# The first weight load of a decode block: 32 rows by four instead of sixteen by eight

## The chip, the core and the metric

The kernel runs on one core of a Trainium2 chip. Five engines work on their own instruction streams: TensorE (PE; its weight loads are shown apart as PEld), VectorE (DVE), ScalarE (ACT), GpSimd (POOL) and SyncE (SP), which here issues nearly all transfers. Sixteen DMA engines move data between the device memory and the core's on-chip memory of 128 partitions; one transfer is shared out over them in packets. The metric is the device time of one execution in microseconds (us), as the median of several runs.

## What is computed

One decode step for eight sequences: normalisation of x, attention over the last 2,048 positions of a cache (32 query heads, 8 key/value heads of 128), and a gated feed-forward block whose output gates the attention's.

```python
x  = A_x                                   # 8 x 1 x 512, bf16
xn = layernorm(x)
W  = min(4096, max(256, Sk // 4))          # Sk = 8192: W = 2048
q  = xn @ wq                               # wq: 512 x 4096, 32 heads of 128
k, v = the last W rows of the caches       # caches: 8 x 8 x 8192 x 128
p  = softmax(q k^T / sqrt(128))
s  = (p v) @ wo                            # wo: 4096 x 512
h  = sigmoid(xn @ w_gate) * (xn @ w_up)    # 512 x 1792 each
g  = silu(h @ w_down)                      # 1792 x 512
out = x + s * g
```

## The kernel before

All loads but that of x go through one helper (lines 112 to 115) and so through SP's queue, in program order; x comes in three pieces on ScalarE's queue (line 125). SP waits only where a load reuses a buffer. K tiles, the weights of the feed-forward block and wo share a ring of three buffers, V tiles a ring of four; `issue_loads` (line 216) issues the next load of a list ordered by when its tile is due, as soon as the buffer before it has been released.

The order on SP's queue is: wq (two loads, lines 131 and 132), K 0 and K 1 at once, K 2 when the q projection has released wq's buffer, then the other K loads (eight of 4 MB in all), the V loads (sixteen of 2 MB), gate and up weights, the down weight, and wo in six pieces that get smaller.

wq is 512 x 4096 in bf16: 8 KB a row. Its first 128 rows are contraction tile 0 and come in the first load, one row to a partition. The other 384 rows come in the second load, three adjacent rows to a partition. Which row stands on which partition is free, as long as normed x is brought into the same order. Line 131 cuts the first 128 rows into 8 by 16 and swaps them, so that partition 8e+i takes row 16i+e. The transfer's source then has 16 outer rows, 8 KB apart, by 8 inner rows, 128 KB apart, of 8 KB each; the destination is 128 partitions.

Normed x (8 x 512, `xn_bf`) is built on VectorE and ScalarE from line 244 on, after x has landed. Lines 265 to 269 copy its first 128 columns into `xn0_bf` in the order of the partitions; for the other contraction tiles a strided view is enough. Four PE transposes (line 272) put the columns on partitions, line 297 copies them into `xnT_sb`, and `q_projection` (line 412) multiplies: two groups of 16 matmuls (line 421), contraction tile 0 first. So the first four matmuls need the first load alone, the fifth needs the second load.

From there `q_out` brings q into the block form `qz_sb` (ScalarE and VectorE, lines 435 to 452). A loop over steps (line 685) then runs, each with its own lag: VectorE's 32x32 transposes of K tiles in place (line 480, 64 of them), the score matmuls (line 495), maxima, exponentials on ScalarE, the turning and spreading of the probabilities, and the products with V (line 625). Near the end come the feed-forward block (lines 370 and 396) and the output projection with wo (line 739), which consumes wo's pieces as they land, then two VectorE instructions and the store.

The K loads have a source of 32 outer rows by 4 (lines 144 to 149: sequence and head by a quarter of the rows), the V loads too (lines 160 to 165: 32 groups of rows by 4 heads). The second wq load, gate, up, down and wo have 128 outer rows, one to a partition.

Of the kernel before, what the change touches and what calls it, by code (L numbers as in the profile page):

```python
# [10 lines left out]
def kernel(  # L11
# [14 lines left out]
    P = 128  # L26
# [85 lines left out]
    def load(dst, src, q=None):  # L112
        if q is None:
            q = nc.sync
        q.dma_start(out=dst, in_=src)  # L115

    def k_tile(shape, name):
        return kring.tile(shape, bf16, name=name, tag="kring", align_bytes=ALIGN)
# [5 lines left out]
    for c0, c1 in ((0, 2), (2, 3), (3, 4)):  # L124
        nc.scalar.dma_start(
            out=x_bf[:, P * c0 : P * c1],
            in_=A_x.flatten_outer_dims()[:, P * c0 : P * c1],
        )

    wq_sb = k_tile([P, KT, Hq * Dh], "wq_sb")  # L130
    load(wq_sb[:, 0], A_wq[:P].rearrange("(i e) n -> e i n", e=16))
    load(
        wq_sb[:, 1:].rearrange("p kt n -> p (kt n)"),
        A_wq[P:].rearrange("(p kt) n -> p (kt n)", kt=KT - 1),
# [81 lines left out]
    def issue_loads():  # L216
# [36 lines left out]
        out=rstd[:], in_=mv[:, 1:2], func=AF.Sqrt, bias=eps_t[:], scale=1.0  # L253
    )
    nc.vector.reciprocal(out=rstd[:], in_=rstd[:])
    xn_bf = ppool.tile([B, D], bf16, name="xn_bf", tag="pp")
    nc.vector.tensor_scalar(
        out=xn_bf[:],
# [5 lines left out]
    )  # L264
    xn0_bf = work.tile([B, P], bf16, name="xn0_bf")
    nc.vector.tensor_copy(  # L266
        out=xn0_bf[:].rearrange("b (e i) -> b e i", e=16),
        in_=xn_bf[:, :P].rearrange("b (i e) -> b e i", e=16),
    )
    xnT_ps = psum_a.tile([P, KT, B], bf16, name="xnT_ps", tag="acc_ps")  # L270
    for kt in range(KT):
        nc.tensor.transpose(  # L272
            out=xnT_ps[:, kt, :],
            in_=xn0_bf[:] if kt == 0 else xn_bf[:B, P + kt - 1 :: KT - 1],
# [3 lines left out]
    for kt in range(KT):  # L278
        nc.tensor.transpose(
            out=xnU_ps[:, kt, :], in_=xn_bf[:B, kt::KT], identity=ident[:B, :B]  # L280
        )
    x2_ps = psum1.tile([NCOL * 32, DC], f32, name="x2_ps", tag="misc")
    for c in range(NCOL):
# [21 lines left out]
        out=HR[:],  # L305
        in_=ident[:].rearrange("m (h q r) -> m h r q", q=NQ, r=rep),
# [6 lines left out]
        out=Qm[:],  # L313
        in_=ident[:].rearrange("m (h q r) -> m q h r", q=NQ, r=rep),
# [6 lines left out]
        out=Hm[:],  # L321
        in_=ident[:].rearrange("p (a gl) -> p gl a", gl=GL),
# [6 lines left out]
    for j in range(GL):  # L329
        for gg in range(NG):  # L330
            g = NG * gg + j // 2
            nc.gpsimd.tensor_copy(
                out=spread[:, gg, j % 2, :, j], in_=ident[:, 32 * g : 32 * g + PP]
# [5 lines left out]
        out=rows_of[:],  # L339
        in_=ident[:].rearrange("p (a m) -> p m a", m=w),  # L340
# [5 lines left out]
        out=Sel[:], in_=rows_of[:].rearrange("p (g c r) -> p c g r", g=GL, c=NCH)  # L346
# [5 lines left out]
    for gg in range(NG):  # L352
        rows = slice(32 * gg, 32 * (gg + 1))
        cols = slice(NE * GL * rep * gg, NE * GL * rep * (gg + 1))
        for e in range(NE):
            nc.gpsimd.tensor_copy(
                out=pick[rows, e, cols].rearrange("p (h d) -> p h d", d=NE)[:, :, e],
                in_=ident[rows, 32 * gg : 32 * gg + GL * rep],
# [326 lines left out]
    for t in range(PV_LAG + NSLOT):  # L685
# [18 lines left out]
        if u >= NJ and u % NJ == 0:  # L704
            i = u // NJ - 1
# [47 lines left out]
    for c in range(NCOL):  # L753
        queues[c].dma_start(
            out=out.flatten_outer_dims()[:, DC * c : DC * (c + 1)],
            in_=y_bf[32 * c : 32 * c + B, :],
# [31 lines left out]
```

## Time and profile before

| | |
|---|---|
| time, median of 3 runs (us) | 199.28 (199.24, 199.28, 204.17) |
| the profiled execution (us) | 199.27 |
| its span, first to last instruction (us) | 197.5 |
| mean TensorE clock granted | 0.912 |
| PE busy | 102.0 us, 52% of the span |
| VectorE busy | 105.7 us, 53% |
| ScalarE busy | 30.9 us, 16% |
| GpSimd busy | 4.7 us, 2% |
| read from device memory | 81.01 MB, 410 GB/s over the span |
| first wq load (1 MB), issue to landing | 7.0 us |
| second wq load (3 MB), issue to landing | 13.5 us |
| K loads (4 MB each), median | 20.1 us |

How to read the profile: times in it are from the span's start. The page cuts the span into 40 slices and gives for each the busy tenths of every engine, the granted TensorE clock, the DMA engines' busy share and what they moved. The chain follows the work that ended last back to the start. The view of windows gives, for stretches of one's own choice, each engine's busy time with the number of its instructions, then the granted clock, the DMA share and GB/s; packets are counted where they start, so short windows can show shares over 1. The list of queues gives packets, MB and the time of the packets as a share of 16 engines. The time from issue to landing of a load contains its wait behind the loads ahead of it in the queue.

### The profile page before, as it was taken

Reading aid. Unit: us, or ns where it says so; the run is one execution under the profiler, and the core shown is the slowest. Engines: PE = TensorE matmul, PEld = TensorE weight load, DVE = VectorE, ACT = ScalarE, POOL = GpSimd, SP = SyncE. Lnnn points to the kernel's source line nnn. Section 1 sums busy time; section 2 is a strip of 40 time slices with the busy share of each in tenths; the row PEclk is TensorE's granted clock in tenths of the full one; section 3 lists DMA queues with packets and bytes.
Section 4 is the critical chain, followed back from the end, with each engine's and each line's share of the span. In section 5 each row is a group of like instructions: output and inputs, shape, how many; then the busy total and the mean of one; then the engine's idle time right before and its main releaser. Section 6 shows DMA issues by size and latency. Waiting matters only on the chain.

```text
span 197.5 us, 1899 instructions
## 1 busy us (share of the span) xinstructions
PE 102.0 (52%) x754; PEld 36.0 (18%) x754; DVE 105.7 (53%) x150; ACT 30.9 (16%) x70; POOL 4.7 (2%) x26
## 2 busy tenths in 40 slices
PE   0026003333333327423495989848634894596653
PEld 0012001110101112100021222322211231233551
DVE  0244199998999999799969924423100010040401
ACT  2004132000000073200011034421111114002000
POOL 8000000000000000000000000000000000000000
PEclk9999999999999999955579799999999798569999
DMA  5999999999999999899999999999999999999991
GB/s 142 365 450 425 425 425 425 425 428 418 433 504 431 431 425 425 378 445 448 425 428 425 425 425 428 446 435 425 435 425 425 428 427 433 444 421 422 433 396 36
DMA packets 5128, 81.14 MB, mean 411 GB/s; under 512 B 616, under 2 KB 768, under 8 KB 1152
## 3 DMA queue, kind: packets, MB, share of 16 engines
q1 hardware_dynamic: 5056, 81.01, 96.8%
q8 instruction: 6, 0.10, 0.2%
q10 hardware_dynamic: 64, 0.01, 0.0%
q14 instruction: 2, 0.02, 0.0%
HBM read 81.01 MB, written 0.01 MB: 410 GB/s over the span
## 4 chain that ended last, share of the span: by engine, by line
DMA 63%; DVE 23%; PE 10%; SPq 1%; issue 1%; ACT 1%; DVEq 0%
DMA k_sb<-in_A_k_cache_dram 25%; DVE k_sb L480 18%; DMA wgu_sb<-in_B_w_up_dram 13%; DMA wo_sb<-in_A_wo_dram 12%; DMA v_sb<-in_A_v_cache_dram 7%; DMA wq_sb<-in_A_wq_dram 7%; PE acc_ps L625 3%; DVE pt_bf L543 2%; PE pT_ps L556 2%; PE o_ps L651 2%; PE q_ps L421 2%; PE s_ps L495 1%; DVE mx L509 1%; SPq L115 1%; DVE o_sb L660 0%
## 5 line engine op out<-in xcount | busy, mean ns | idle before, releaser
L480 DVE STREAM_TRANSPOSE k_sb<-k_sb 128x1024 f32<-128x1024 f32 x64 | 73.7, 1209 | 6.4 <-DMA k_sb<-in_A_k_cache_dram 6.3
L495 PE MATMUL s_ps<-k_sb,qz_sb 128*32 128x512 bf16 x256 | 30.1, 570 | 53.7 <-DVE k_sb L480 47.9
L625 PE MATMUL acc_ps<-v_sb,pT_sb 128*64 128x512 bf16 x256 | 37.3, 421 | 10.9 <-DMA v_sb<-in_A_v_cache_dram 10.7
L660 DVE TENSOR_TENSOR o_sb<-o_ps,rden 16x512 bf16<-16x512 f32 (+2 forms) x6 | 3.0, 504 | 47.4 <-PE o_ps L651 47.4
L495 PEld LDWEIGHTS <-qz_sb 128*32 128x32 bf16 x256 | 8.6, 116 | 78.3 <-issue 55.2
L639 ACT COPY acc_sb<-acc_ps 128x512 f32<-128x512 f32 x16 | 9.4, 585 | 82.5 <-PE acc_ps L625 82.5
L625 PEld LDWEIGHTS <-pT_sb 128*64 128x64 bf16 x256 | 12.7, 116 | 30.9 <-DMA v_sb<-in_A_v_cache_dram 15.4
L651 PE MATMUL o_ps<-acc_sb,Sel 128*16 128x512 f32 (+2 forms) x48 | 16.5, 494 | 3.4 <-ACT acc_sb L639 3.4
L577 DVE TENSOR_SCALAR pT_sb<-pc_bf,Hm 128x1024 bf16<-128x1024 bf16 x16 | 6.6, 477 | 5.3 <-PE acc_ps L625 5.3
L523 ACT ACT_TABLE_LOAD x1 | 1.3, 1283 | 39.8 <-DVE nm L517 39.8
L651 PEld LDWEIGHTS o_ps<-acc_sb,Sel 128*16 128x16 f32 x48 | 4.7, 105 | 14.4 <-issue 8.1
L509 DVE TENSOR_REDUCE mx<-s_ps 128x1 f32<-128x512 f32 x8 | 5.3, 662 | 3.2 <-PE s_ps L495 3.2
L556 PE MATMUL pT_ps<-pt_bf,spread 128*128 128x512 bf16 x16 | 6.0, 500 | 1.2 <-DVE pt_bf L543 0.7
L739 PE MATMUL a_ps<-wo_sb,o_sb 128*32 128x256 bf16 x64 | 4.5, 273 | 3.6 <-DMA wo_sb<-in_A_wo_dram 3.4
L452 ACT COPY qz_sb<-qT_sb 32x32 bf16<-32x32 bf16 x20 | 4.8, 242 | 8.1 <-DVE qT_sb L440 7.9
L370 PE MATMUL d_ps<-wgu_sb,xnU_sb 128*32 128x448 bf16 x32 | 3.4, 573 | 4.9 <-DMA wgu_sb<-in_B_w_up_dram 2.6
L272 PE MATMUL xnT_ps<-ident,xn_bf 8*128 8x8 bf16 x4 | 0.3, 167 | 10.9 <-DVE xn_bf L266 10.9
L523 ACT ACTIVATE p_bf<-s_ps,nm 128x512 bf16<-128x512 f32 x8 | 5.4, 685 | 0.0
L421 PE MATMUL q_ps<-wq_sb,xnT_sb 128*32 128x512 bf16 x32 | 3.8, 626 | 2.9 <-DMA wq_sb<-in_A_wq_dram 2.9
L564 ACT CAST pc_bf<-pT_ps 128x512 bf16<-128x512 f32 x8 | 4.5, 586 | 5.0 <-DVE pt_bf L543 2.8
L543 DVE STREAM_TRANSPOSE pt_bf<-p_bf 128x512 bf16<-128x512 bf16 x8 | 4.9, 666 | 0.0
L244 DVE CAST x_f<-x_bf 8x512 f32<-8x512 bf16 x1 | 0.4, 415 | 8.1 <-DMA x_bf<-in_A_x_dram 8.1
(64 smaller groups left out, 40.3 us busy)
## 6 DMA issues: line engine op xcount, KB each, us to landing
k_sb<-in_A_k_cache_dram SPq DMA_DIRECT2D x8, 4096.0 KB, 20.1
v_sb<-in_A_v_cache_dram SPq DMA_DIRECT2D x16, 2048.0 KB, 16.1
wq_sb<-in_A_wq_dram SPq DMA_DIRECT2D x1, 3072.0 KB, 13.5
wgu_sb<-in_B_w_gate_dram SPq DMA_DIRECT2D x1, 1792.0 KB
wgu_sb<-in_B_w_up_dram SPq DMA_DIRECT2D x1, 1792.0 KB, 24.7
wd_sb<-in_B_w_down_dram SPq DMA_DIRECT2D x1, 1792.0 KB
wo_sb<-in_A_wo_dram SPq DMA_DIRECT2D x1, 1536.0 KB
wo_sb<-in_A_wo_dram SPq DMA_DIRECT2D x1, 1152.0 KB, 33.4
```

Of the source, the lines that this page charges most:

```text
L421: nc.tensor.matmul(q_ps[gg][32 * gl : 32 * (gl + 1), :], lhsT=xnT_sb[:, kt, :], rhs=wq_sb[:, kt, h0 : h0 + HW], start=(kt == 0), stop=(kt ...
L452: nc.scalar.copy(out=out, in_=in_)
L480: nc.vector.transpose(out=kw, in_=kw)
L495: nc.tensor.matmul(s_tiles[i][32 * g : 32 * (g + 1), :], lhsT=qz_sb[:, hb, h, 2 * a + e, :], rhs=kT[:, :, a, h, :, e], start=(n == 0), sto ...
L509: nc.vector.reduce_max(out=mx_of[hb][:, kq : kq + 1], in_=s_tiles[i][:], axis=AX.X)
L523: nc.scalar.activation(out=p_bf[:, :, kq], in_=s_tiles.pop(NK * hb + kq)[:].rearrange("p (o c j) -> p c j o", o=2, j=NC), func=AF.Exp, bia ...
L543: nc.vector.transpose(out=pt[:, w * n : w * (n + 1)], in_=p_bf[:, w * n : w * (n + 1)])
L556: nc.tensor.matmul(pT_ps[:], lhsT=spread[:, gg, y].rearrange("p k g -> p (k g)"), rhs=pt[:, c, y, :], start=(y == 0), stop=(y == 1), skip_ ...
L577: nc.vector.tensor_scalar(out=pT_of[hb, gg][:, :, gl, :], in0=pc, scalar1=Hm[:, gl : gl + 1], scalar2=None, op0=ALU.mult,)
L625: nc.tensor.matmul(acc_tiles[i][w * c : w * (c + 1), :], lhsT=pT[:, GL * rep * ch : GL * rep * ch + w], rhs=v_tiles[i][:, ch : ch + NCH, : ...
L639: nc.scalar.copy(out=acc_sbs[i // NSUM][:, i % NSUM], in_=acc_tiles.pop(i)[:])
L651: nc.tensor.matmul(o_ps[rows, :n, :], lhsT=Sel[:, c].rearrange("p g r -> p (g r)"), rhs=acc_sb[:, :, Dh * c : Dh * (c + 1)], start=(c == 0 ...
```

## The change

Two numbers go from 16 to 32. The first wq load cuts its 128 rows into 4 by 32 before it swaps them: partition 4o+i takes row 32i+o, and the source has 32 outer rows, 8 KB apart, by 4 inner rows, 256 KB apart. `xn0_bf` is written in the same order. The bytes, the size of a row, the number of instructions and the order of all work stay as they are; each engine's instructions stand in the same order in both programs.

```diff
     wq_sb = k_tile([P, KT, Hq * Dh], "wq_sb")
-    load(wq_sb[:, 0], A_wq[:P].rearrange("(i e) n -> e i n", e=16))
+    load(wq_sb[:, 0], A_wq[:P].rearrange("(i e) n -> e i n", e=32))
     load(
         wq_sb[:, 1:].rearrange("p kt n -> p (kt n)"),
...
     xn0_bf = work.tile([B, P], bf16, name="xn0_bf")
     nc.vector.tensor_copy(
-        out=xn0_bf[:].rearrange("b (e i) -> b e i", e=16),
-        in_=xn_bf[:, :P].rearrange("b (i e) -> b e i", e=16),
+        out=xn0_bf[:].rearrange("b (e i) -> b e i", e=32),
+        in_=xn_bf[:, :P].rearrange("b (i e) -> b e i", e=32),
     )
```

## The prediction

> **What bounds the kernel now.** I read the page's slices first, then its chain and its list of transfers.
>
> ```profile
> DMA  5999999999999999899999999999999999999991
> GB/s 142 365 450 425 425 425 425 425 428 418 433 504 431 431 425 425 378 445 448 425 428 425 425 425 428 446 435 425 435 425 425 428 427 433 444 421 422 433 396 36
> ...
> q1 hardware_dynamic: 5056, 81.01, 96.8%
> ...
> DMA 63%; DVE 23%; PE 10%; SPq 1%; issue 1%; ACT 1%; DVEq 0%
> ...
> wq_sb<-in_A_wq_dram SPq DMA_DIRECT2D x1, 3072.0 KB, 13.5
> ...
> wq_sb<-in_A_wq_dram SPq DMA_DIRECT2D x1, 1024.0 KB, 7.0
> ```
>
> The 16 DMA engines are full from the first slices to the last but one, on one queue. PE and VectorE stand at 52 and 53% of the span. So the end is set by bytes over rate, and a hole at the start of the stream moves everything after it. The only slices well under 425 GB/s while the queue has work are the first two: there lies the load that the change touches, 1 MB that lands 7.0 us after its issue.
>
> Then the stages, cut where that load's packets go round (one round is one packet on each of 16 engines). The last two columns are the DMA share and GB/s.
>
> ```profile
> 2.38:2.74 0.36, 0.00 (x0) 0.00 (x0) 0.00 (x0) 0.36 (x1) 0.30 (x2) 1.00 1.19 364
> 2.74:3.19 0.45, 0.00 (x0) 0.00 (x0) 0.00 (x0) 0.45 (x1) 0.45 (x4) 1.00 0.96 328
> 3.19:3.67 0.48, 0.00 (x0) 0.00 (x0) 0.00 (x0) 0.15 (x1) 0.48 (x5) 1.00 1.05 274
> 3.67:4.27 0.60, 0.00 (x0) 0.00 (x0) 0.00 (x0) 0.00 (x0) 0.54 (x4) 1.00 1.06 221
> 4.27:4.90 0.63, 0.00 (x0) 0.00 (x0) 0.00 (x0) 0.00 (x0) 0.59 (x5) 1.00 0.94 208
> 4.90:5.46 0.56, 0.00 (x0) 0.00 (x0) 0.00 (x0) 0.00 (x0) 0.53 (x4) 1.00 1.19 278
> 5.46:6.04 0.58, 0.00 (x0) 0.00 (x0) 0.00 (x0) 0.00 (x0) 0.00 (x0) 1.00 0.94 198
> 6.04:6.55 0.51, 0.00 (x0) 0.00 (x0) 0.00 (x0) 0.00 (x0) 0.00 (x0) 1.00 1.02 209
> 6.55:7.90 1.35, 0.00 (x0) 0.00 (x0) 0.00 (x0) 0.00 (x0) 0.00 (x0) 1.00 0.97 293
> 7.90:8.80 0.90, 0.00 (x0) 0.00 (x0) 0.67 (x2) 0.00 (x0) 0.00 (x0) 1.00 1.01 437
> ...
> 14.25:33.60 19.35, 5.08 (x44) 1.76 (x44) 11.95 (x23) 6.00 (x22) 0.00 (x0) 1.00 1.00 434
> ```
>
> What to see: the engines are busy throughout (share near 1), so nothing waits for an issue; the packets themselves are slow. The load starts near 364 GB/s, falls to 221 and 208, has one better stretch (278) just past its middle, and falls again; the 3 MB load behind it is slow for one more round and then runs at 437. A cold start would be slow first and quick later; this is the reverse, as if what takes the data in runs at half speed once the room ahead of it is full. The queue's packets (packets, MB, share of 16 engines) in three windows, 3.6 to 6.5, 7.9 to 14.25 and 14.28 to 24.0 us, give the time of one:
>
> ```profile
> q1 hardware_dynamic: 80, 0.66, 103.9%
> ```
>
> ```profile
> q1 hardware_dynamic: 112, 2.75, 100.6%
> ```
>
> ```profile
> q1 hardware_dynamic: 146, 4.23, 100.7%
> ```
>
> First load: 1.039 x 16 x 2.9 / 80 = 0.60 us for 8 KB. Second wq load: 1.006 x 16 x 6.35 / 112 = 0.913 us for 24 KB, so 0.304 for 8 KB. First K load (146 less 17 four-byte packets): 1.007 x 16 x 9.72 / 129 = 1.214 us for 32 KB, again 0.303 for 8 KB. The slow load moves at half the rate of the others, and it alone has a source of 16 outer rows by 8. The second wq load has 128 rows. All K and V loads have 32 by 4: the form that the change gives to the first load. Both run full from their first packets.
>
> **The change part by part.** No instruction is added, removed or reordered on any engine: the same 1,024 KB in 128 rows of 8 KB, the same issue on SP, the same copy of normed x on VectorE with other strides.
>
> (1) The first load in 32 by 4. The stream's first packet starts at 2.39 us, the first K packet at 14.29 us, with the 4.19 MB of both wq loads between (1.05 + 0.39 + 2.75 MB). At the 434 GB/s of the K stage they take 9.66 us; they took 11.90. So 2.24 us are lost, and that is the most that the load can give back. Bound from below: the gain is nothing if the new form keeps 0.60 us a packet, and negative if packets get slower still (rival D). I take nearly the full gain, because the rows of the same form (K, V) are the nearest: what I leave out is the ramp of the first round, whose packets take about 0.43 us instead of 0.305 even before the room is full, and some overlap of the start, together some 0.2 us. That leaves 2.05 us.
>
> [...]
>
> (2) Whether the gain reaches the end. The queue never runs dry: at each later issue I took the bytes issued so far, less those of finished packets, over 432 GB/s; the least backlog is 6.2 us (K loads issued at 57.3 and 66.9 us). Those issues wait for VectorE's transposes and PE's matmuls, which themselves follow the landings and move with them; even if they did not move, 6.2 us covers 2.05. So the stream stays closed, and every landing, the last wo piece at 193.77 us and the 3.7 us behind it move by the full amount. VectorE begins its K transposes at 24.66 us on the first K landing; that moves to 22.6, and it is the transfer that is late next, as before.
>
> (3) Copy of normed x (line 266).
>
> ```profile
> 10.55 0.26 DVE L266 COPY xn_bf<-xn_bf 8x128 bf16<-8x128 bf16 x1
> ...
> 11.52 0.62 PE L421 MATMUL q_ps<-wq_sb,xnT_sb 128*32 128x512 bf16 x4
> ...
> 15.03 3.18 PE L421 MATMUL q_ps<-wq_sb,xnT_sb 128*32 128x512 bf16 x28 [2.90 <-DMA wq_sb<-in_A_wq_dram]
> ```
>
> Its inner runs become four long instead of eight. Bounds: 0.06 us (the smallest VectorE instruction of this stretch) and 0.41 us (the cast of 8x512), so -0.20 to +0.15; I take 0. It lies on the chain x, norm, transpose, first four q matmuls, which ends at 12.14 us; PE then waits 2.90 us for the second wq load. After the change that load lands near 12.97, so 0.8 us of the cover are left. Were it gone, PE's 3.2 us of q matmuls would start later by the excess; behind them stand the second half of q on ScalarE and VectorE, the first score matmuls, and SP's third K issue, which has 15.8 us of backlog ahead of it. So it costs nothing at the end. The same holds if the x rows, whose packets are slipped between those of wq on the same engines, land up to a round of 24 KB (0.9 us) later.
>
> (4) The issue on SP: 0.67 us before, 0.58 to 0.61 for the K loads of the new form. It stands ahead of the first packet, so up to 0.09 us could be gained or lost; I take 0.
>
> Sum: 199.27 us (this execution's own time: 197.5 of span and 1.77 around it) - 2.05 = 197.2. The median of the runs shown is 199.28, so nothing is to be corrected.
>
> **The rivals.**
> A, the forecast: the load runs at full rate, 197.2 us, between 196.9 (all 2.24 us and the issue's 0.09) and 197.6 (the first two rounds stay as they are, about 0.2 us more, and some of the x traffic).
>
> B, half the gain: engines collide in part of the steps, or the first rounds of any stream are slow. For it: already the packets before 3.2 us average some 0.4 us, before anything is full. Against it: the K form runs full from its first packet, though it follows a running stream. Eight packets at 0.45 us are 3.6 instead of about 4.3 us, with some of the second load's slow round: 1 us, 198.2 us.
>
> C, the change does not do what it says: the slowness belongs to the first megabyte or to the start of the program, or the new rows are dealt to the engines as before. For it: no other load is the first one, and no other has 8 KB packets. Against it: quick at first and slow later, and packets of 1 to 14 KB near the end run within a few per cent of the full rate. 199.3 us.
>
> D, slower, on the memory's side: an engine's successive rows are 256 KB apart instead of 128, and the engines no longer read sixteen adjacent rows at a time. If the reads then collide, it costs eight packets: it decides once a packet takes over 0.535 us on average (4.28 / 8); at 0.80, between the slow 0.60 and the 1.21 of four engines on one resource, the load takes 6.4 instead of 4.28 us: 201.4. To be 4 us slower it needs 1.03 us. Against it: K rows in step lie 2 MB apart and run at 1.214 us for 32 KB. [...]
>
> **How the numbers follow.** A 0.75, B 0.08, C 0.12, D 0.05. The time is A's, 197.2. The range 196.9 to 198.6 holds A but for a few hundredths and B: 0.8; it leaves out C and D. About 2% (4 us) is what a measurement of this kernel tells from no change. A's largest gain is 2.3 us, so faster by over 2% gets 0.01; slower by over 2% is the far end of D, 0.03; within 2% is the rest, 0.96.
>
> **What would show it.** Right: wq's first load lands near 5.8 instead of 7.8 us, its 8 KB packets average near 0.31 to 0.35 us with no fall to 210 GB/s, PE's second group of q matmuls starts near 13.0 instead of 15.03, K transposes near 22.6 instead of 24.66, and the last wo piece releases PE near 191.7. Wrong: the same 200 to 220 GB/s between 3.6 and 6.5 us (C), packets over 0.54 us (D), or a gap in the DMA stream later on that eats the gain (then step 2 failed).

## The result and the profile after

The changed kernel takes 198.10 us (median of five, 197.69 to 198.42) against 199.31 before; the ratio is 0.9939, with a 95% interval of 0.9923 to 0.9955. The profiled execution takes 198.13 us with a span of 196.4, against 199.27 and 197.5. So it gained 0.6% (about 1.2 us), where 2.05 us were forecast. The time lies in the range, 0.9 us above the point. Some executions take several us longer throughout (204.17 us once before the change); they are left out of every ratio, and since the trace kept of one experiment, e3, is of such an execution (203.67 us, K packets of 1.36 instead of 1.21 us), no packet time of it is compared.

The page of the changed kernel, the lines that answer to the first ones shown of before:

```profile
DMA  5999999999999999899999999999999999999990
GB/s 190 436 444 427 427 427 441 441 431 422 434 447 447 434 441 427 380 424 474 427 397 437 434 424 431 439 427 431 424 427 427 434 432 431 433 425 423 430 378 24
...
wq_sb<-in_A_wq_dram SPq DMA_DIRECT2D x1, 3072.0 KB, 12.0
...
wq_sb<-in_A_wq_dram SPq DMA_DIRECT2D x1, 1024.0 KB, 5.4
```

The first slice moved from 142 to 190 GB/s and the second from 365 to 436; the later slices scatter around the same rate as before. The first load lands 1.6 us earlier after its issue (5.4 for 7.0), the second 1.5 us (12.0 for 13.5). The stages, cut at the same times as before:

```profile
2.38:2.74 0.36, 0.00 (x0) 0.00 (x0) 0.00 (x0) 0.36 (x1) 0.30 (x2) 1.00 1.14 296
2.74:3.19 0.45, 0.00 (x0) 0.00 (x0) 0.00 (x0) 0.45 (x1) 0.45 (x4) 1.00 1.08 309
3.19:3.67 0.48, 0.00 (x0) 0.00 (x0) 0.00 (x0) 0.14 (x1) 0.48 (x5) 1.00 0.48 171
3.67:4.27 0.60, 0.00 (x0) 0.00 (x0) 0.00 (x0) 0.00 (x0) 0.54 (x4) 1.00 0.88 371
4.27:4.90 0.63, 0.00 (x0) 0.00 (x0) 0.00 (x0) 0.00 (x0) 0.59 (x5) 1.00 0.99 417
...
7.90:8.80 0.90, 0.00 (x0) 0.00 (x0) 0.54 (x2) 0.29 (x1) 0.00 (x0) 1.00 1.01 437
14.25:33.60 19.35, 4.36 (x40) 1.45 (x33) 13.42 (x24) 5.99 (x22) 0.00 (x0) 1.00 1.01 434
```

The stretches at 221 and 208 GB/s are gone: 371 and 417. The first three rows did not get better (296, 309 and 171 GB/s for 364, 328 and 274): the load starts no faster than before. (A window counts a packet where it starts. So 171 is in part a matter of counting, and between 4.9 and 7.9 us, where the second load's packets of 24 KB begin in bunches, the rows jump between 228 and 733; such rows are read over several windows.) In the trace the 8 KB packets from the fourth round on take 0.31 us on average, as was forecast for the right case; the first three rounds take 0.39, 0.48 and 0.46 us (0.43, 0.37 and 0.49 before).

How far the gain travels, in instructions of the changed kernel:

```profile
13.53 3.18 PE L421 MATMUL q_ps<-wq_sb,xnT_sb 128*32 128x512 bf16 x28 [2.96 <-DMA wq_sb<-in_A_wq_dram]
...
23.20 2.37 DVE L480 STREAM_TRANSPOSE k_sb<-k_sb 128x1024 f32<-128x1024 f32 x2 [3.99 <-DMA k_sb<-in_A_k_cache_dram]
```

and in its chain:

```profile
169.12 23.52 DMA wo_sb<-in_A_wo_dram
192.63 0.04 issue
192.67 0.63 PE a_ps L739 x6
```

PE's second group comes 1.50 us earlier (15.03 before), VectorE's first K transposes 1.46 us (24.66), and the wo piece that the chain waits for last 1.14 us (193.77). That is the fifth of the six wo pieces, which the prediction calls the last; the sixth lands 0.33 us later in both kernels. The gain shrinks on the way, though no gap opened in the stream. The last stretches, before:

```profile
190.00:191.00 1.00, 0.28 (x6) 0.28 (x7) 0.00 (x0) 0.00 (x0) 0.00 (x0) 1.00 0.91 371
191.00:192.00 1.00, 0.88 (x17) 0.69 (x13) 0.00 (x0) 0.00 (x0) 0.00 (x0) 1.00 1.01 399
192.00:193.00 1.00, 0.72 (x10) 0.53 (x10) 0.00 (x0) 0.00 (x0) 0.00 (x0) 1.00 0.68 250
193.00:194.00 1.00, 0.69 (x10) 0.50 (x10) 0.00 (x0) 0.00 (x0) 0.00 (x0) 1.00 0.26 95
```

and after:

```profile
190.00:191.00 1.00, 0.69 (x14) 0.50 (x9) 0.00 (x0) 0.00 (x0) 0.00 (x0) 1.00 0.99 375
191.00:192.00 1.00, 0.72 (x10) 0.53 (x10) 0.00 (x0) 0.00 (x0) 0.00 (x0) 1.00 0.39 146
192.00:193.00 1.00, 0.83 (x10) 0.52 (x10) 0.00 (x0) 0.00 (x0) 0.00 (x0) 1.00 0.11 38
```

What to see is the share, the column before GB/s. It does not drop from 1 to 0: the engines finish one after another, and the tail is 0.39 and then 0.11 (less than two engines of 16), where it was 0.68 and 0.26. These windows do not end at the same distance from the last landing; counted back from it, the last two microseconds have 0.62 and 0.22 before, 0.40 and 0.12 after. In the trace the middle landing of the sixth wo piece's sixteen shares (one for each DMA engine) comes 1.41 us earlier than before, the last one 1.14. So two questions: is the form of the load what made it slow, and where did the rest of the gain go?

### The profile page after: what moved, and what is told of

It is laid out like the page before. It is cut to its first block, busy times and chain, and to the rows that moved or that the text cites. A ratio compares the mean times of both kernels' runs of the same rounds, so it can differ in the third digit from the quotient of the medians.

```text
span 196.4 us, 1899 instructions
## 1 busy us (share of the span) xinstructions
PE 103.0 (52%) x754; PEld 36.4 (19%) x754; DVE 105.7 (54%) x150; ACT 30.9 (16%) x70; POOL 4.7 (2%) x26
## 4 chain that ended last, share of the span: by engine, by line
DMA 63%; DVE 23%; PE 10%; SPq 1%; issue 1%; ACT 1%; DVEq 0%
DMA k_sb<-in_A_k_cache_dram 25%; DVE k_sb L480 18%; DMA wgu_sb<-in_B_w_up_dram 13%; DMA wo_sb<-in_A_wo_dram 12%; DMA v_sb<-in_A_v_cache_dram 7%; DMA wq_sb<-in_A_wq_dram 6%; PE acc_ps L625 3%; DVE pt_bf L543 2%; PE pT_ps L556 2%; PE o_ps L651 2%; PE q_ps L421 2%; PE s_ps L495 1%; DVE mx L509 1%; SPq L115 1%; DVE o_sb L660 0%
## 5 line engine op out<-in xcount | busy, mean ns | idle before, releaser
L625 PE MATMUL acc_ps<-v_sb,pT_sb 128*64 128x512 bf16 x256 | 39.5, 443 | 10.7 <-DMA v_sb<-in_A_v_cache_dram 10.6
L625 PEld LDWEIGHTS <-pT_sb 128*64 128x64 bf16 x256 | 13.4, 121 | 31.4 <-DMA v_sb<-in_A_v_cache_dram 14.5
L651 PE MATMUL o_ps<-acc_sb,Sel 128*16 128x512 f32 (+2 forms) x48 | 15.8, 475 | 3.4 <-ACT acc_sb L639 3.4
L739 PEld LDWEIGHTS <-o_sb 128*32 128x32 bf16 x64 | 3.5, 96 | 3.1 <-issue 3.0
```

Of the source, the lines that this page charges most:

```text
L625: nc.tensor.matmul(acc_tiles[i][w * c : w * (c + 1), :], lhsT=pT[:, GL * rep * ch : GL * rep * ch + w], rhs=v_tiles[i][:, ch : ch + NCH, : ...
L651: nc.tensor.matmul(o_ps[rows, :n, :], lhsT=Sel[:, c].rearrange("p g r -> p (g r)"), rhs=acc_sb[:, :, Dh * c : Dh * (c + 1)], start=(c == 0 ...
L739: nc.tensor.matmul(a_ps[32 * c : 32 * (c + 1), :], lhsT=o2_sb[:, k, :], rhs=wo_parts[k][:, DC * c : DC * (c + 1)], start=(k == 0), stop=(k ...
```

## Experiments

All runs come with runs of the kernel before on the same chip; a ratio is to those. Theories: F, the form of 16 outer rows makes the engines collide where the data goes in; M, the order in which the memory's rows are read decides; S, the start of the program is slow, whatever is loaded.

| run | edit | us | ratio (95%) |
|---|---|---|---|
| e1 | first load in plain order | 197.50 | 0.9908 (0.9894 to 0.9921) |
| e2 | first load 64 by 2 | 197.76 | 0.9922 (0.9909 to 0.9936) |
| e3 | 16 by 8, other rows | 199.66 | 1.0015 (1.0006 to 1.0024) |
| e4 | second load 16 by 8 | 205.24 | 1.0289 (1.027 to 1.0308) |
| e5 | e1, 64 KB more for one engine at the start | 198.70 | 0.9962 (0.9947 to 0.9977) |
| e6 | e1, the same over 16 engines | 198.52 | 0.9946 (0.9927 to 0.9966) |
| e7 | wq in one load | 197.58 | 0.9908 (0.9893 to 0.9922) |
| e8 | second load 32 by 4 | 198.01 | 0.9925 (0.991 to 0.994) |
| e9 | e5, issued behind K 1 | 198.98 | 0.9973 (0.9963 to 0.9983) |
| e10 | e6, issued behind K 1 | 198.20 | 0.9957 (0.9932 to 0.9982) |
| e11 | the changed kernel again, one run | 197.57 | |
| e12 | e1's first load in two halves | 199.91 | 1.0019 (1.001 to 1.0028) |

### The form, the rows or the start (e1 to e4, e8)

e1, on the changed kernel:

```diff
-    load(wq_sb[:, 0], A_wq[:P].rearrange("(i e) n -> e i n", e=32))
+    load(wq_sb[:, 0], A_wq[:P])
...
-        out=xn0_bf[:].rearrange("b (e i) -> b e i", e=32),
-        in_=xn_bf[:, :P].rearrange("b (i e) -> b e i", e=32),
+        out=xn0_bf[:],
+        in_=xn_bf[:, :P],
```

> The first wq load in the plain order of the rows (partition p takes row p, 128 outer rows), normed x not reordered. Theory F (the form of the load: 16 outer rows put the DMA engines in each other's way on the side that takes the data in, 32 or 128 do not): 8 KB packets at 0.31 us after the first three rounds, as in the changed kernel, 198.1 us within 0.3. Theory M (the order in which the memory's rows are read decides): here the engines read rows some 32 KB apart instead of adjacent ones, another order than both kernels had, so the packets should take another time than 0.31 us, 0.4 to 0.6, 198.6 to 199.5 us. Theory S (the start of the program is slow, and the change helped for another reason): not told apart from F here.

197.50 us: full rate, 382 to 437 GB/s where the kernel before had 328 falling to 208:

```profile
2.74:3.19 0.45, 0.00 (x0) 0.00 (x0) 0.00 (x0) 0.45 (x1) 0.45 (x4) 1.00 1.05 382
3.19:3.67 0.48, 0.00 (x0) 0.00 (x0) 0.00 (x0) 0.12 (x1) 0.48 (x5) 1.00 1.03 427
3.67:4.27 0.60, 0.00 (x0) 0.00 (x0) 0.00 (x0) 0.00 (x0) 0.54 (x4) 1.00 1.05 437
```

It lies below F's range (197.8 to 198.4). Its stream also starts sooner: SP's first issue takes 0.41 us instead of 0.65 in the changed kernel, the first packet begins at 1.78 us instead of 2.20 (2.39 before), and the first K packets at 12.24 on average, where the changed kernel has 12.74 and the kernel before 14.41. M expected another packet time than 0.31 us; it is 0.31 to 0.33 from the fourth round on.

e2 has e=64 in the same two places.

> The first wq load with 64 outer rows by 2 (partition 2o+i takes row 64i+o). F: still full rate, 0.31 us for 8 KB, 198.1 us within 0.3, if more outer rows are dealt to the engines as 32 are. If instead outer rows were dealt so that an engine's successive rows change their place with the number of outer rows, packets of 0.45 to 0.6 us and 198.5 to 199.3 us. M: an engine's rows are 512 KB apart now; if pitch matters, slower than 0.31 us a packet.

197.76 us, just under F's range, and 0.31 us a packet from the fifth round on: 64 outer rows run full here as 32 did (0.31 us), and rows 512 KB apart cost nothing.

e3 brings the slow form back, on other rows:

```diff
-    load(wq_sb[:, 0], A_wq[:P].rearrange("(i e) n -> e i n", e=32))
+    load(wq_sb[:, 0], A_wq[: 9 * 16].rearrange("(e i) n -> e i n", e=16)[:, :8])
```

> The first wq load in the form of the kernel before, 16 outer rows by 8, but of other rows: each engine's eight rows are adjacent (8 KB apart) and the engines are 72 KB apart. It reads rows 9e to 9e+7 of Wq, which are not those that the reference multiplies, so only its time counts. F: slow as before, 0.60 us a packet from the fourth round on with a better stretch just past the middle, 199.3 us. M: the order is quite another than before (16 adjacent rows at a time, 128 KB apart in one engine), so the packets leave 0.60 us by more than a tenth; full rate would give 198.1.

199.66 us: as slow as the kernel before, even 0.15% slower. The rows are read in quite another order and nothing improves: spread over eight rounds, the 0.33 us are 0.04 us a packet, within the tenth that M had to leave. This rests on the time alone. By it M falls for this load.

e4 (and e8 with 32 for 16) changes the second load:

```diff
-        A_wq[P:].rearrange("(p kt) n -> p (kt n)", kt=KT - 1),
+        A_wq[P:].rearrange("(i e kt) n -> e i (kt n)", kt=KT - 1, e=16),
...
+    for kt in range(1, KT):
+        nc.vector.tensor_copy(
+            out=xn1_bf[:, kt - 1].rearrange("b (e i) -> b e i", e=16),
+            in_=xn_bf[:, P + kt - 1 :: KT - 1].rearrange("b (i e) -> b e i", e=16),
+        )
```

> The changed kernel with its second wq load (3 MB) put in 16 outer rows by 8, in packets of 24 KB; normed x's other columns are copied into that order by three more small VectorE copies. F: its packets take 1.8 instead of 0.91 us, eight rounds of 0.9 us more, so about 7 us later at the first K landing and at the end: 205 us. S (only the first traffic is slow): 0.91 to 1.0 us a packet, 198.1 to 198.5 us. M: between the two.

> The control for e4: the second wq load in 32 outer rows by 4, with the same three extra copies of normed x. F: its 24 KB packets take 0.91 us as in the changed kernel, 198.1 us within 0.4. If e4's loss came from the reordered rows or the copies and not from the 16 outer rows, it stays at 203 us or more.

205.24 and 198.01 us, both as F had it. The windows of e4, then of e8:

```profile
3.60:4.60 1.00, 0.00 (x0) 0.00 (x0) 0.00 (x0) 0.00 (x0) 0.94 (x7) 1.00 1.02 428
7.00:18.00 11.00, 1.73 (x14) 0.76 (x15) 3.67 (x17) 0.74 (x3) 0.00 (x0) 1.00 0.98 203
21.60:30.00 8.40, 2.81 (x28) 0.90 (x20) 3.11 (x11) 3.10 (x10) 0.00 (x0) 0.88 1.01 437
```

```profile
6.30:12.70 6.40, 1.71 (x14) 0.75 (x15) 3.95 (x17) 0.74 (x3) 0.00 (x0) 1.00 1.04 445
```

In e4 the first load runs at 428 GB/s, the second, in the form of 16 outer rows, at 203 with the engines just as busy (0.98), and K behind it at 437. The slow place moved from the first load to the second, so it belongs to the form and not to the start: S falls. e8 has the same copies and a rearranged source too, and 445 GB/s.

### What of the form (e12)

```diff
-    load(wq_sb[:, 0], A_wq[:P])
+    load(wq_sb[:64, 0], A_wq[:64])
+    load(wq_sb[64:, 0], A_wq[64:P])
```

> The kernel of e1 (plain order, 197.5 us) with its first wq load cut in two loads of 64 rows, to partitions 0 to 63 and then 64 to 127, one row to a partition; no form of 16 outer rows is left. Theory F in its narrow form (the form of 16 outer rows is slow as such): full rate, 0.31 us for 8 KB, 197.5 to 197.8 us with one more issue. Theory P (what collides is where the data goes in: 64 adjacent partitions offer the 16 engines half the room that 128 do): about 0.6 us for 8 KB in both halves once the room ahead is full, with a better stretch in the middle where the first engines pass to the second half, as in the kernel before: 198.8 to 199.5 us.

199.91 us: slow, with no 16 outer rows anywhere. That is 0.4 us above P's range and over 2 us above F's; the pattern is the kernel before's:

```profile
2.74:3.19 0.45, 0.00 (x0) 0.00 (x0) 0.00 (x0) 0.45 (x1) 0.45 (x4) 1.00 0.88 309
3.19:3.67 0.48, 0.00 (x0) 0.00 (x0) 0.00 (x0) 0.17 (x1) 0.48 (x5) 1.00 1.32 307
3.67:4.27 0.60, 0.00 (x0) 0.00 (x0) 0.00 (x0) 0.00 (x0) 0.54 (x4) 1.00 1.03 207
4.27:4.90 0.63, 0.00 (x0) 0.00 (x0) 0.00 (x0) 0.00 (x0) 0.59 (x5) 1.00 0.98 223
4.90:5.46 0.56, 0.00 (x0) 0.00 (x0) 0.00 (x0) 0.00 (x0) 0.53 (x4) 1.00 1.03 234
```

In the trace its eight rounds take 0.71, 0.37, 0.52, 0.64, 0.59, 0.55, 0.62 and 0.64 us, those of the kernel before 0.43, 0.37, 0.49, 0.62, 0.60, 0.54, 0.62 and 0.64. So F in its narrow form falls, and P fits: two loads to 64 adjacent partitions each run at 207 to 234 GB/s from 3.67 us on, where e1's one load to 128 has 437. The author's reading is that the rate depends on which partitions the 16 engines write at one time. That a source of 16 outer rows has them write only half of the partitions at any time is the one reading that fits e3, e4 and e12 together, but no record names the engine or the partition of a packet, so that link stays an inference. Nor does a run split the load into halves of other partitions, so that it is the partitions and not the split as such rests on the pattern being the same.

### Where the rest of the gain went (e5, e6, e9 to e11)

Theory L: each engine works off its own share of the stream, none takes over from another, and the end waits for the last one. B: the stream's bytes over its mean rate set the end. e5 and e6 put 64 KB more, that nobody reads, on ScalarE's queue at the start of e1; they differ in how these are laid over partitions:

```diff
+    extra = v_tile([P, CH, Dh], "extra")
+    for n in range(4):
+        nc.scalar.dma_start(
+            out=extra[n : n + 1].rearrange("p c d -> p (c d)"),
+            in_=A_wo[16 * n : 16 * (n + 1)].rearrange("(o r) n -> o (r n)", o=1),
+        )
```

(e6: `out=extra[16 * n : 16 * (n + 1), :4]`, 16 rows of 1 KB, and `in_` without the rearrangement.)

> The kernel of e1 (plain order, 197.5 us) with 64 KB more to load at the start that nobody reads: four rows of 16 KB into one partition each, on ScalarE's queue behind x, each a transfer of one row that one DMA engine carries, the same one for all four as I expect. Theory L (every engine works off its own share of the stream, none takes over another's, and the end waits for the one that is last): 64 KB are 2.4 us for that engine at 27 GB/s; the last engine of e1 is some 1.4 us behind the middle one from the program fetches, so the end comes 1.0 us later if that engine gets no program fetch of its own and 2.4 us later if it does: 198.5 to 199.9 us. Theory B (the stream's bytes over its mean rate set the end): 64 KB in 81 MB are 0.15 us: 197.65 us.

> As e5, with the same 64 KB spread over all 16 engines: four transfers of 16 rows of 1 KB, each into a partition of its own. L and B both: 4 KB more per engine, 0.15 to 0.2 us: 197.7 us within 0.2. Were e5's extra time the issue of four more transfers and not the one engine, it would show here too.

198.70 and 198.52 us. The first lies in L's range, but the second misses its own by 0.6, and the difference between them decides nothing: four more issues at that place disturb the start itself. The first K packets of e6 begin at 12.84 us on average instead of e1's 12.24, those of e5 at 12.48. Inconclusive in time. So e9 and e10 issue the same on SP, behind K 1 (`load(...)` for `nc.scalar.dma_start(...)`, after the first `issue_loads()`).

> The kernel of e1 (plain order, 197.5 us) with 64 KB more that nobody reads, four rows of 16 KB for one DMA engine, now issued on SP behind the first two K loads, so that the start of the stream is left as it is (in e5 and e6 the start was disturbed, by 0.2 and 0.6 us at the first K packets). Theory L (each engine works off its own share, the end waits for the last one): 2.4 us on one engine; the last engine of e1 is about 1.4 us behind the middle one from a program fetch, so the end comes 1.0 us later if the loaded engine gets no program fetch, up to 2.4 us if it does: 198.5 to 199.9 us, and the last landings of K 2 and after lie 2.4 us behind the middle ones. Theory B (bytes over the mean rate): 0.15 us, 197.65 us.

> As e9, with the same 64 KB spread over 16 engines, four transfers of 16 rows of 1 KB, issued at the same place. L and B: 4 KB more per engine at 46 ns per 1 KB, 0.2 us: 197.7 us within 0.25. L is told from B by the difference between e9 and this run: 0.8 us or more against none.

198.98 and 198.20 us: 0.78 us between them, just short of the 0.8 named. e10 lies 0.7 us over e1, where 0.2 was expected, and 0.25 above its range; two of its ten executions (199.76 and 200.17) lie above all of e9's. The traces tell what of this is the stream's. The last wo landing comes at 193.07 us in e9, at 192.35 in e10 and at 192.39 in e1. From the store's issue to the end of the span it is 2.57 and 2.52 us in e9 and e10 for 2.27 in e1, and the time around the span is 2.2 us for 1.8. So e10's stream ends no later than e1's, and its 0.7 us lie behind the stream and around the span; why four more loads cost that there is not shown. e9's stream ends 0.7 us later than either. L's sum had 1.0, and B's 0.15 is out. The last windows, of e9:

```profile
191.00:192.00 1.00, 0.72 (x10) 0.53 (x10) 0.00 (x0) 0.00 (x0) 0.00 (x0) 1.00 0.30 111
192.00:193.00 1.00, 0.71 (x10) 0.51 (x10) 0.00 (x0) 0.00 (x0) 0.00 (x0) 1.00 0.05 18
```

of e10:

```profile
191.00:192.00 1.00, 0.70 (x10) 0.32 (x7) 0.00 (x0) 0.00 (x0) 0.00 (x0) 1.00 0.33 120
192.00:193.00 1.00, 0.62 (x6) 0.29 (x5) 0.28 (x1) 0.00 (x0) 0.00 (x0) 1.00 0.00 0
```

In e9's last stretch the share is 0.05, less than one engine of 16: a single one still works, and PE waits for it. The landings of the engines' shares in the trace say the same: K 2's middle share lands at 41.81 us and its last at 44.23; K 5, 29 us later, at 70.89 and 73.23; so the engine keeps its 2.3 to 2.4 us. To the end of the kernel this is plainest against the first landing: the last share is 2.61 us behind it at K 2 and 2.62 at the sixth wo piece. So no other engine took work off it in this run.

This is also how the changed kernel lost part of its gain. Its first K packets begin within 0.6 us of each other, one engine 0.42 us behind the middle; before, all lay within 0.23 us. From 42 us on (41.92 us here, 43.39 before) the program itself is fetched, in six packets of 16 KB:

```profile
q8 instruction: 6, 0.10, 0.2%
```

(This line of the page is the same before and after.) Followed by the start times of its packets, since the records do not name it, an engine that carries such a piece falls back by some 1.4 us and stays there: before, with fetches at 43.39 and 84.60 us, the last landing of the V load that comes next (V 0) is 1.47 us behind the middle one. In the changed kernel the fetch at 82.87 us meets the engine that was late already: in the landings a lag of 0.34 us disappears and one of 1.92 us takes its place. The last landing of that V load comes 1.08 us earlier than before, the middle one 1.53.

e11 is the changed kernel once more, unaltered.

> The changed kernel once more, for a second look at its start. L: the spread of the engines after the first load (0.8 us from first to last landing in the first look, 0.3 in the kernel before) and which of them a program fetch delays differ from run to run, so the time lies anywhere between 197.5 and 198.5 us, and the last landings lie behind the middle ones by 1.4 us or more. If the spread were fixed by the form of the load, 0.8 us again and the same engine last.

197.57 us, in the range of L: the engines' first landings lie within 0.3 us, not 0.8, the latest at the first K packets is 0.28 us behind, the last landing lies 1.2 to 1.8 us behind the middle one from K 2 on (L had named 1.4 or more), and the fifth wo piece lands at 192.06 us, 1.71 us earlier than before. The form does not fix the spread. This execution had gained 1.84 us at the first K packets and keeps all but 0.13 of it; the execution profiled above had 1.67 and lost 0.53.

### One load for all of wq (e7)

```diff
-    load(wq_sb[:, 0], A_wq[:P].rearrange("(i e) n -> e i n", e=32))
...
+        A_wq.rearrange("(p kt) n -> p (kt n)", kt=KT),
...
-            in_=xn0_bf[:] if kt == 0 else xn_bf[:B, P + kt - 1 :: KT - 1],
+            in_=xn_bf[:B, kt::KT],
```

> All of wq in one load of 128 rows of 32 KB (partition p takes rows 4p to 4p+3), no reordering copy; q's first four matmuls no longer start before the rest has landed, some 0.6 us of PE that lie beside transfers. F: full rate from the start, no second issue ahead of the stream; 0.1 to 0.3 us less than e1's 197.5 through fewer, larger packets: 197.3 us within 0.3. If the small first load were needed to get the stream going early, 197.7 or more.

197.58 us: no better than e1. Its first round takes 1.80 us instead of 1.21 for 32 KB, so what the first packets lose does not go away with larger ones. e1 and e7 beat the kernel before by 0.9%, with fewer instructions in e7. They stand below the changed kernel's 0.9939 too, with intervals that do not overlap, though the changed kernel's further run (197.57) reaches them.

## Why the prediction held, and where it did not

**The bound.** Right: the stream of transfers sets the end. Only the rate of a 1 MB load changed, with no engine's work, and the end moved (the last wo landing by 1.14 us, the span from 197.5 to 196.4).

**Step 1, the mechanism.** Right as far as the runs reach: e4 moves the slow place with the form, e3 keeps the loss with other rows, e12 makes it with 64 partitions. How 16 outer rows put the engines on half of the room is argued, not shown, and which rows an engine reads one after the other is the author's reading of each load's form. Rivals C and D are out: D's wider pitches cost nothing in the changed kernel (256 KB) or in e2 (512 KB), both at 0.31 us a packet after the first rounds; and C, which had the 200 to 220 GB/s stay, falls with the changed kernel's 371 and 417. D's 1.21 us for four engines on one resource was an estimate, four times the 0.303 us of the full rate; no run shows four engines so placed, and the form of 16 outer rows took 0.60 us.

**Step 1, the size.** This term was too large. "I take nearly the full gain" left out 0.2 us for the ramp. Measured at the first K packets the gain is 1.67 us (14.41 to 12.74 on average) instead of 2.05, and 0.21 of it is no rate at all: the first packets begin at 2.29 us on average for 2.50. Step 4 held this to 0.09, and e4, with the same first load, begins at 2.51, so it is not shown to come from the change. The two loads themselves gave 1.46 us. The first three rounds of the new form still take 0.39, 0.48 and 0.46 us, 0.4 us more than three full ones. Rival B had that half right, and the time is B's 198.2 rather than A's 197.2; that the packets then run full, with no fall to 210 GB/s, is A's sign. So the range held the result partly because it was drawn to hold B as well. The first round was slower than a full one in every run (0.33 to 0.81 us on average for 8 KB), and how slow differs from run to run, with the same load too (0.33 in e1, 0.81 in e10); why stays open.

**Step 2, "move by the full amount".** This step failed. The stream did stay closed and the backlog did cover the shift, as it said; but a closed stream was taken for one resource, and it is 16. The last engine's gain counts: 1.46 us at the first K transposes, 1.14 at the end, where the middle engine has 1.41, because the engines start further apart and a program fetch fell on a late one. Some 0.2 us that the middle engine itself loses between K 1 and K 3 (its landings come 1.75, then 1.55 us earlier) stay open; packets of 32 KB there take up to 1.31 us instead of 1.21, besides those that share an engine with a fetch. How much this step loses is partly luck: 0.53 us in the execution profiled first, 0.13 in e11, which still misses the 2.05 by the size of step 1.

**Steps 3 and 4.** Right in their costs. The copy on line 266 takes 0.26 us as before. The x rows came sooner too, so the first four q matmuls start at 9.95 instead of 11.52 us and PE waits 2.96 us for the second load; the cover did not shrink to 0.8. The issue takes 0.65 instead of 0.67 us.

## What to carry to other kernels

Where the DMA engines are busy and the rate is half, look at how the transfer's rows are laid over the partitions: one row to each of 128 partitions, or 32 outer rows by four, ran full here (0.30 to 0.31 us for 8 KB); 16 by eight and halves of 64 partitions ran at half (about 0.6 us). A saving at the head of a full stream was worth what the last engine saved (1.14 us at the end), not the middle one (1.41): read the last windows' share, and the last landing beside the middle one, before the whole of it is counted.

## What the runs showed that was not expected

A fetch of 16 KB of program cost the engine that carried it about 1.4 us for good, more than the 0.6 us that 16 KB of V take: before the change, the last share lies 0.10 us behind the middle one at K 1, 1.62 at K 2, after the first fetch, and still 1.33 at the sixth wo piece. And sixteen engines at full rate did not always start evenly: the first load's landings lie within 0.3 us of each other before the change and in e2, 0.8 in e1, 0.8 and 0.3 in two runs of the changed kernel. Whether the slow load itself kept the engines together is not shown.
